# Attention with mixture of experts on one core: values of the last 64 queries in the same PSUM tile as those before, and two key chunks ahead of them

## The chip, the cores and the metric

The kernel runs on one core of one Trainium2 chip. The metric is the device time of one execution in microseconds; lower is better. Matrix work runs on TensorE (PE), with its weight loads shown as PEld; VectorE is DVE, ScalarE is ACT, GpSimd is POOL, and SP issues most of the DMAs.

## The reference

Everything is float32. There are 4 batches of 8 heads, 576 tokens and head dimension 64.

```python
scores = scale * np.matmul(q, k.transpose(0, 1, 3, 2))
bias = np.maximum((psi_rel / psi_i)[..., None] @ w1 + b1, 0.0) @ w2
scores = scores + bias.transpose(2, 0, 1)[None, :, :, :]
attn = softmax(scores)                  # over the keys, written out with max, exp and sum
x = np.matmul(attn, v)                  # then laid out as 2304 tokens by 512
e_idx = np.argmax(x @ w_gate, axis=1)   # one expert of 8 for each token
for e in range(8):
    h = np.maximum(x[mask] @ w1[e], 0.0)
    out[mask] = gate_w[mask, None] * eom[mask, e, None] * (h @ w2[e])
```

## The kernel before, in words

The program has three stages: the bias table, which the first pair of heads already overlaps; attention over 16 pairs of heads (a pair is a batch `b` and two heads `pr`, 4 pairs to a batch); and the experts. Attention is software pipelined over pairs. A loop over `n` from 0 to 16 reads a string of short operation names, and each name emits instructions on several engines in that order. `FIRST` is the string of n = 0, `ORDER` that of n = 1 to 14, `LAST` that of n = 15, `END` that of n = 16. Every engine then executes its own instructions strictly in the order of emission, so the string is the schedule. A name with `-` works on pair n-1, with `+` or `++` on pair n+1 or n+2.

The names that matter here:

- `s0` to `s7` (`emit_s`, scores): query block and head, two blocks of 288 keys. Four matmuls (L853) write a tile `ps`; DVE adds the bias and finds the row maximum (L833); ACT takes the exponential into a tile `e` (L838). `s5` and `s4` are the last scores of a pair, `s2` and `s1` the first of the next. `s8` is the same for the 64 queries that are left (L869).
- `t..` (`emit_t`): transposes of `e` on PE (L890, and L902 for the last 64 queries) into a tile `pt`, then a copy to SBUF. The last letter of a name tells the engine of the copy, `a` for ACT and `d` for DVE; in the last batch t00, t01, t04 and t14 are copied by ACT. In the part that changes these are `t14` (2 transposes), `t13` and `t00` (4 each) and `t21` (1, L902).
- `a0`, `a1`, `a2` (`emit_av`, values): `a0` and `a1` have 256 queries each, `a2` the last 64. Each is 20 matmuls (L922), 64 columns of the array wide, in two interleaved groups of partitions 0 to 63 and 64 to 127, into a tile `pa`, then one copy by ACT or DVE (L923).
- `k0`, `k1`, `k2` (`emit_kq`, key and query chunks of pair n+2): three transposes (L803) into `pt`, then ACT writes the rounded high part `hi` (L806), then DVE the low part `lo` from `pt` and `hi` (L808). Only then is `pt` free.
- `p0` to `p2` (`emit_place`): DMAs on SP that put `hi` and `lo` of pair n+1 where the scores need them (L819). `l` and `v` load keys, queries and values; `z` and `g` are small POOL copies.
- `w` and `u` (`do_work`): one step of the work that waits in a list, namely the gate logits of a finished batch (L586, L616, L628), its routing (small DVE and POOL operations), and the output rows (`emit_x`, 4 transposes L655 into `pt` and a DVE multiplication L664). `u` counts only from n = 12. A `w` step can be empty.

The pools: `ps` has 2 buffers, `pt` has 3 that are used in turn by all of `t`, `k` and the list's steps, and `pa` has one:

```python
ps_t = ctx.enter_context(tc.tile_pool(name="ps_t", bufs=3, space=PSUM))
ps_s = pool("ps_s", 2, space=PSUM)
ps_a = pool("ps_a", 1, space=PSUM)
```

Of the kernel before, what the change touches and what calls it, by code (L numbers as in the profile page):

```python
# [9 lines left out]
F32 = mybir.dt.float32  # L10
# [10 lines left out]
B, H, S, D = 4, 8, 576, 64  # L21
HID = 32
NPAIR = H // 2
# [22 lines left out]

ORDER = (
    "s2 s1 c w u a0d- t10a- p0+ s3 u w t11a- s0 u t12a- s6 t20d- p1+ u s7 b- t04d u s8 t01d t03a u "
    "t02a s5 s4 z+ u w w g- a1a- t14d u p2+ t13a t00d u k0++ a2a- v+ t21d u k1++ w k2++ u l+++ "
)  # L50

FIRST = (
# [82 lines left out]
def attention_moe_kernel(  # L135
# [15 lines left out]
    nc = tc.nc  # L151
# [404 lines left out]
    work = []  # L556
# [17 lines left out]
    def xt_of(b, qq):  # L574
        if (b, qq) not in xt_t:
            n = 256 if qq < 2 else 64
            nm = f"xt{int(qq == 2)}"
            xt_t[b, qq] = xt_p.tile([128, NPAIR, n], F32, name=nm, tag=nm, bufs=4 if qq < 2 else 2)
        return xt_t[b, qq]
# [92 lines left out]
    with ExitStack() as actx:  # L672
# [167 lines left out]
        def emit_s(b, pr, qb, hl):  # L840
            h = 2 * pr + hl
            if b not in sums_t:
                sums_t[b] = st_p.tile([128, 4, H], F32, name="sums", tag="sums", bufs=2)
                sums4_t[b] = st_p.tile([128, NPAIR], F32, name="sums4", tag="sums4", bufs=2)
            e_t[b, pr, qb] = e_all[qb]
            ps = ps_s.tile([128, 2, 512], F32, name="ps", tag="s")
            kt, qs = (x[(b * NPAIR + pr) % 2] for x in (kh2, qs2))
            low = kl_t[b, pr]
            o = hl * S + qb * 128
            k0 = hl * S  # L850
            for c in range(2):
                for n, keys in enumerate((kt, low)):
                    nc.tensor.matmul(  # L853
                        ps[:, c, 0:288], lhsT=qs[:, o:o + 128], rhs=keys[:, k0 + c * 288:k0 + c * 288 + 288],
                        start=n == 0, stop=n == 1,
                    )
            yield
            softmax_rows(e_t[b, pr, qb][:, hl, :], ps, bias[qb][:, h, :], sums_t[b][:, qb, h:h + 1])
# [45 lines left out]
                )  # L904
            copy(out=et[0:m, n0 * 128:(n0 + nn) * 128], in_=pt[0:m, 0:nn * 128])

        def emit_av(b, pr, qq, copy):
            et = et_t.pop((b, pr, qq))
            n = 256 if qq < 2 else 64
            vt, z = v_t[b, pr], vz[(b * NPAIR + pr) % 2]  # L910
            pa = ps_a.tile([128, 256], F32, name="pa", tag="a")
            if qq < 2:
                first = [(vt[:, i, :], et[:, i, :]) for i in range(4)] + [(z[:, 0, :], et[:, 4, :])]
                second = [(vt[:, 5 + i, :], et[:, 5 + i, :]) for i in range(4)] + [(z[:, 1, :], et[:, 4, :])]
            else:
                first, second = (
                    [(x[:, i, :], et[:, i, o:o + 64]) for i in range(4)] + [(y, et[:, 4, o:o + 64])]
                    for x, y, o in ((vt, z[:, 0, :], 0), (vb_t.pop((b, pr)), vz[2], 64))
                )
            for i in range(5):  # L920
                for p, (values, weights) in zip((0, 64), (first[i], second[i])):
                    nc.tensor.matmul(pa[p:p + 64, 0:n], lhsT=values, rhs=weights, start=i == 0, stop=i == 4)  # L922
            copy(out=xt_of(b, qq)[:, pr, :], in_=pa[:, 0:n])  # L923

        pairs = [(b, pr) for b in range(B) for pr in range(NPAIR)]
        begun = " ".join(BEGIN.values()).split()
# [20 lines left out]
        def finish(g):  # L947
            for _ in g:
                pass
# [44 lines left out]
        def copies(c):  # L994
            return nc.scalar.copy if c == "a" else V.tensor_copy
# [5 lines left out]
        for n in range(len(pairs) + 1):  # L1001
            todo = {i: 1 for i in range(8)}
            for op in orders.get(n, ORDER).split():
                name = op.rstrip("+-")
                m = n + op.count("+") - op.count("-")
                if name == "w":
                    do_work()
                elif name == "u" and n >= len(pairs) - NPAIR:
                    do_work((work,))
                elif name == "x":  # L1010
                    transpose_x(0, chunks.pop(0))
                elif name == "W":
                    first_w1()
                elif name == "B":
                    emit_load_vb(*pairs[-1])
                elif name == "X":
                    while any(w.__name__ == "route_group" for w in work):
                        do_work((work,))
                    first_x()
                elif name == "y":  # L1020
                    first_split(splits.pop(0))
                if name in "wuxWBXy" or not 0 <= m < len(pairs) or m == 0 and name in begun or m == 1 and name[0] == "p":
                    continue
                b, pr = pairs[m]
                i = int((name + "0")[1])
                if name == "s8":
                    emit_s4(b, pr)
                elif name[0] == "s":
                    finish(emit_s(b, pr, i // 2, i % 2))
                    if m == len(pairs) - 1:  # L1030

                        todo.pop(i)
                        if i > 5 and not any(j in todo for j in (6, 7)):
                            work.insert(0, first(first_w2))
                        if i in (4, 5) and not any(j in todo for j in (4, 5)):
                            t = biasp.tile([128, 4, 4, CH], F32R, name="x", tag="bias2")
                            xs.update({j: (t[:, 2 * j], t[:, 2 * j + 1]) for j in range(2)})
                elif name[0] == "t":
                    emit_t(
                        b, pr, i, int(name[2]), copies("a" if name[0:3] in to_act and b == B - 1 and m < len(pairs) - 1 else name[3])  # L1040
                    )
                elif name[0] == "a":
                    emit_av(b, pr, i, copies(name[2]))
                    if i == 2 and m == len(pairs) - 2:
                        emit_zb(*pairs[-1])
                    if pr == NPAIR - 1:
                        work.append(emit_logits(b, i))
                        if i == 2:
                            work.append(emit_route(b))
                            if b >= B - 2:  # L1050
                                work.append(route_group(b - (B - 2)))
                elif name[0] in "kp":
                    if name[0] == "p":
                        emit_place(b, pr, i)
                    else:
                        finish(emit_kq(b, pr, i))
                else:
                    {"l": emit_load, "v": emit_load_v, "c": emit_z, "b": emit_load_vb, "g": emit_zb, "z": emit_q4}[name](b, pr)
# [204 lines left out]
```

## Time and profile before

| | us |
|---|---|
| median of 3 runs | 620.95 |
| lowest and highest | 619.73, 623.54 |
| profiled execution | 615.56 |
| its span, first to last instruction | 613.4 |
| its mean granted PE clock, share of full speed | 0.987 |

The profile is of one execution, 615.56 us long, of which 613.4 us are the span and 2.16 us lie around it. Times in the rows are microseconds from the span's start. The matmul ends shown are modelled and overlap the next starts, so in this text a step on PE is measured from one start to the next start. A row `x10` merges ten neighbouring instructions of one kind.

### The profile page before, as it was taken

To read this page: it belongs to the slowest core of one execution; us is meant where nothing else is said; L and a number is where in the kernel's file an instruction comes from. 1 tells how busy PE (TensorE), PEld (TensorE's weight loads), DVE (VectorE), ACT (ScalarE), POOL (GpSimd) and SP (SyncE) were. 2 spreads that over 40 slices of the span, in tenths; PEclk is the share of its full clock that TensorE was granted. 3 is DMA by queue.
4 is the path that set the end of the run, shared out by engine and by line. 5 is a ranking of instruction groups with operands and counts; after the bars stand their busy time and mean duration, and the time that the engine had idled before them with its cause. 6 is when DMAs were issued, how large, how long until landed. Compare 5 with 4: busy or idle time off the path is not lost.

```text
span 613.4 us, 13534 instructions
## 1 busy us (share of the span) xinstructions
PE 575.6 (94%) x5070; PEld 489.3 (80%) x5070; DVE 413.5 (67%) x974; ACT 374.8 (61%) x774; POOL 94.9 (15%) x172
## 2 busy tenths in 40 slices
PE   4878789999999999999999999999999999999993
PEld 2333478887887788887778769999999999999993
DVE  6968656676786677786579765766777675555621
ACT  5778667777775677776776664545545454545410
POOL 1000000000001000100012383040404132220202
PEclk9979989999999999999999999999999999999998
DMA  6998975655656745676436686576656574855521
GB/s 144 226 207 207 215 161 116 139 125 108 143 127 169 167 99 108 137 184 157 105 88 158 185 263 198 172 221 204 202 179 203 172 221 145 241 166 182 174 71 47
DMA packets 99094, 100.26 MB, mean 163 GB/s; under 512 B 71320, under 2 KB 71576, under 8 KB 99017
## 3 DMA queue, kind: packets, MB, share of 16 engines
q1 hardware_dynamic: 93028, 84.93, 54.4%
q0 software_dynamic: 3232, 9.64, 5.0%
q10 hardware_dynamic: 2756, 4.72, 2.2%
q8 instruction: 42, 0.69, 0.5%
q14 instruction: 36, 0.29, 0.2%
HBM read 60.34 MB, written 9.50 MB: 114 GB/s over the span
## 4 chain that ended last, share of the span: by engine, by line
PE 79%; DVE 7%; ACT 5%; DMA 5%; issue 3%; POOL 0%; POOLq 0%; SPq 0%; DVEq 0%; ACTq 0%
PE p L1115 16%; PE p L1138 16%; PE pa L922 13%; PE ps L853 10%; PE pt L890 10%; PE pt L803 2%; DMA bias<-evh 2%; PE pb L735 2%; PE ps L869 2%; DVE e L833 2%; DVE hid L724 2%; PE pt L655 1%; PE pt L1157 1%; PE pt L902 1%; PE pt L515 1%
## 5 line engine op out<-in xcount | busy, mean ns | idle before, releaser
L838 ACT ACTIVATE e<-e,nm 128x576 f32<-128x576 f32 x144 | 111.2, 773 | 49.1 <-DVE nm L833 47.0
L833 DVE CUSTOM_DVE_ANT_0 e<-ps,bias 128x576 f32<-128x576 f32 x144 | 105.6, 751 | 31.3 <-PE ps L853 25.3
L1115 PE MATMUL p<-x,w 128*128 128x288 f32 x768 | 105.8, 297 | 0.0
L1115 PEld LDWEIGHTS p<-x,w 128*128 128x128 f32 x768 | 102.8, 188 | 0.5 <-issue 0.4
L890 PE MATMUL pt<-kept,e 128*128 128x128 f32 x576 | 82.7, 277 | 2.9 <-ACT et L894 1.6
L853 PE MATMUL ps<-qt,qs 128*128 128x288 f32 x256 | 79.9, 331 | 3.2 <-DVE nm L833 3.0
L890 PEld LDWEIGHTS pt<-kept,e 128*128 128x128 f32 x576 | 65.2, 141 | 17.8 <-issue 7.0
L1138 PE MATMUL p<-hh,w2h 128*128 128x288 f32 x256 | 77.4, 302 | 0.0
L1138 PE MATMUL p<-hl,w2h 128*128 128x288 f32 x256 | 75.7, 296 | 0.1
L1138 PE MATMUL p<-hh,w2l 128*128 128x288 f32 x256 | 75.4, 295 | 0.0
L922 PE MATMUL pa<-et,vt 128*64 128x256 f32 (+1 forms) x640 | 73.2, 354 | 0.0
L853 PE MATMUL ps<-kl,qs 128*128 128x288 f32 x256 | 71.3, 296 | 0.0
L894 ACT COPY et<-pt 128x512 f32<-128x512 f32 (+1 forms) x105 | 57.2, 565 | 12.4 <-PE pt L890 12.3
L735 PE MATMUL pb<-hid,w2blk 128*32 128x288 f32 x576 | 47.8, 442 | 17.3 <-DVE hid L724 7.4
L922 PEld LDWEIGHTS pa<-et,vt 128*64 128x64 f32 x640 | 42.6, 137 | 21.8 <-issue 6.0
L853 PEld LDWEIGHTS ps<-qt,qs 128*128 128x128 f32 x256 | 48.9, 191 | 7.2 <-DVE nm L833 4.5
L1117 ACT ACTIVATE hh<-p 128x288 fp32r<-128x288 f32 x64 | 26.3, 411 | 46.1 <-PE p L1115 38.0
L1080 POOL DMA_INDIRECT out_dram<-y,sidx x22 | 26.4, 1198 | 172.9 <-DVE y L1160 145.3
L735 PEld LDWEIGHTS pb<-hid,w2blk 128*32 128x32 f32 x576 | 19.1, 116 | 42.1 <-DVE hid L724 10.7
L724 DVE TENSOR_SCALAR hid<-e,early 128x576 f32<-128x576 f32 x110 | 48.4, 511 | 6.1 <-PE pb L735 2.8
L853 PEld LDWEIGHTS ps<-kl,qs 128*128 128x128 f32 x256 | 49.1, 192 | 0.0
L487 DVE TENSOR_TENSOR w2l<-w2r,w2h 128x1024 fp32r<-128x1024 f32 x32 | 39.2, 1225 | 14.5 <-ACT w2h L486 14.5
(218 smaller groups left out, 970.8 us busy)
## 6 DMA issues: line engine op xcount, KB each, us to landing
w1r<-in_moe_w_dram SPq DMA_DIRECT2D x36, 512.0 KB, 3.7
w2r<-in_moe_w_dram SPq DMA_DIRECT2D x36, 512.0 KB, 4.0
kl<-qs SPq DMA_DIRECT2D x32, 288.0 KB, 5.2
nat<-in_k_dram SPq DMA_DIRECT2D x16, 288.0 KB, 3.9
nat<-in_q_dram SPq DMA_DIRECT2D x16, 288.0 KB, 5.2
bias<-evh SPq DMA_DIRECT2D x16, 288.0 KB, 4.2
bias<-evl SPq DMA_DIRECT2D x16, 288.0 KB, 5.3
qs<-qt SPq DMA_DIRECT2D x16, 288.0 KB, 3.2
```

The source lines that it names most:

```text
L487: V.tensor_tensor(out=lo, in0=src, in1=hi.bitcast(F32), op=ALU.subtract)
L724: V.tensor_scalar(out=to, in0=src, scalar1=bc[:, r:r + 1], scalar2=0.0, op0=ALU.add, op1=ALU.max,)
L735: nc.tensor.matmul(pb[32 * t:32 * t + 32, c, 0:288], lhsT=w2f, rhs=hids[t][:, c * 288:c * 288 + 288], start=True, stop=True,)
L833: V.tensor_tensor_reduce(out=e.rearrange("p (a j) -> p a j", a=2), in0=ps[:, :, 0:n], in1=bias_ap.rearrange("p (a j) -> p a j", a=2), scal ...
L838: nc.scalar.activation(out=e, in_=e, func=ACTF.Exp, scale=-1.0, bias=nm, accum_out=sum_ap)
L853: nc.tensor.matmul(ps[:, c, 0:288], lhsT=qs[:, o:o + 128], rhs=keys[:, k0 + c * 288:k0 + c * 288 + 288], start=n == 0, stop=n == 1,)
L890: nc.tensor.transpose(pt[:, n * 256 + j * 128:n * 256 + j * 128 + 128], es[j][:, (n0 + n) * 128:(n0 + n) * 128 + 128], ident,)
L894: copy(out=et[:, n0:n0 + nn, :].rearrange("p n s -> p (n s)"), in_=pt[:, 0:nn * 256])
L922: nc.tensor.matmul(pa[p:p + 64, 0:n], lhsT=values, rhs=weights, start=i == 0, stop=i == 4)
L1080: p = nc.gpsimd.indirect_dma_start(out=out, out_offset=bass.IndirectOffsetOnAxis(ap=idx, axis=0), in_=y[0:n], in_offset=None, bounds_check ...
L1115: nc.tensor.matmul(p1[:, 0:CH], lhsT=w[:, fs], rhs=x[:, c, :], start=n == 0, stop=n == 11)
L1138: nc.tensor.matmul(p2[:, 0:CH], lhsT=w[f // 2][:, f % 2, ds], rhs=x[f], start=n == 0, stop=n == 23)
```

## The change

The string `ORDER` becomes, where it differs:

```diff
-    "t02a s5 s4 z+ u w w g- a1a- t14d u p2+ t13a t00d u k0++ a2a- v+ t21d u k1++ w k2++ u l+++ "
+    "t02a s5 z+ s4&k0++ k1++ u w w g- a12a- t14d u p2+ t13a t00d u k2++ v+ t21d u w u l+++ "
```

`a12` emits the matmuls of `a1` and then those of `a2`, both into one tile `pa` of 320 columns, and then both copies. `s4&k0` emits the matmuls of `s4`, the transposes and the ACT part of `k0`, then DVE and ACT of `s4`, then the DVE part of `k0`. `k1` follows, and only `k2` stays behind. `FIRST`, `LAST` and `END` stay as they are. At n = 14 there is no pair n+2, and neither kernel has a `k` there.

```diff
-        def emit_av(b, pr, qq, copy):
+        def emit_av(b, pr, qq, copy, pa, at):
             et = et_t.pop((b, pr, qq))
             n = 256 if qq < 2 else 64
             vt, z = v_t[b, pr], vz[(b * NPAIR + pr) % 2]
-            pa = ps_a.tile([128, 256], F32, name="pa", tag="a")
+            pa = pa[:, at:at + n]
...
-                    nc.tensor.matmul(pa[p:p + 64, 0:n], lhsT=values, rhs=weights, start=i == 0, stop=i == 4)
-            copy(out=xt_of(b, qq)[:, pr, :], in_=pa[:, 0:n])
+                    nc.tensor.matmul(pa[p:p + 64], lhsT=values, rhs=weights, start=i == 0, stop=i == 4)
+            yield
+            copy(out=xt_of(b, qq)[:, pr, :], in_=pa)
...
+                op, _, beside = op.partition("&")
...
-                    finish(emit_s(b, pr, i // 2, i % 2))
+                    steps = [emit_s(b, pr, i // 2, i % 2)]
+                    if beside and n + 2 < len(pairs):
+                        steps.append(emit_kq(*pairs[n + 2], int(beside[1])))
+                    for g in steps:
+                        next(g)
+                    for g in steps:
+                        finish(g)
...
-                    emit_av(b, pr, i, copies(name[2]))
...
+                    pa = ps_a.tile([128, 320], F32, name="pa", tag="a")
+                    qqs = [int(c) for c in name[1:-1]]
+                    begun_av = [emit_av(b, pr, i, copies(name[-1]), pa, 256 * j) for j, i in enumerate(qqs)]
+                    for g in begun_av:
+                        next(g)
+                    for i, g in zip(qqs, begun_av):
+                        finish(g)
```

On PE, from the end of `a1` to the next pair's scores at n = 1, the kernel before has these rows; `pt` numbers are single tiles, and what stands in brackets are the engines whose semaphores the row waits for.

```order
L890 MATMUL pt_1185<-kept_93,e0_136 128x128 [waits PE_49]
...
L803 MATMUL pt_1191<-kept_93,nat_1010 128x128 [waits DMAHW5_49,DMAHW4_49,DVE_49]
L803 MATMUL pt_1191<-kept_93,nat_1010 128x128 x2
L922 MATMUL pa_1197<-et4_892,vt_877 64x64 [waits Activation_49]
...
L902 MATMUL pt_1212<-kept_93,e4_891 64x128 [waits Activation_49]
L803 MATMUL pt_1215<-kept_93,nat_1010 128x128 [waits DVE_49]
L803 MATMUL pt_1215<-kept_93,nat_1010 128x128 x2
L803 MATMUL pt_1221<-kept_93,nat_1010 128x128 [waits DVE_49]
L803 MATMUL pt_1221<-kept_93,nat_1010 128x128 x2
L853 MATMUL ps_1230<-qt0_118,qs0_120 128x288 [waits DMAHW3_49,DMAHW0_49]
```

The changed kernel has these there, from `k0` (pt_1156) and `k1` (pt_1165) through the two kinds of values to `t14`, `t13`, `t00`, `k2`, `t21`.

```order
L803 MATMUL pt_1156<-kept_93,nat_1010 128x128 [waits DMAHW5_49,DMAHW4_49,DVE_49]
...
L803 MATMUL pt_1165<-kept_93,nat_1010 128x128 [waits Activation_49]
...
L922 MATMUL pa_1172<-et_977,vt_877 64x256 x8
...
L922 MATMUL pa_1172<-et4_892,vt_877 64x64
...
L890 MATMUL pt_1198<-kept_93,e2_138 128x128 [waits Activation_49]
L890 MATMUL pt_1203<-kept_93,e2_138 128x128 [waits DVE_49]
L890 MATMUL pt_1209<-kept_93,e0_136 128x128 [waits DVE_49]
L803 MATMUL pt_1215<-kept_93,nat_1010 128x128 [waits DVE_49]
L902 MATMUL pt_1223<-kept_93,e4_891 64x128 [waits Activation_49]
L853 MATMUL ps_1229<-qt0_118,qs0_120 128x288 [waits DMAHW3_49,DMAHW0_49]
```

Before, `k2` (pt_1221) takes the buffer of `k0` and waits for its DVE part, and `a2` waits for ACT's copy of `a1`. After, `t13` takes the buffer of `k0`, `t00` that of `k1`, `k2` that of `t14`, and `t21` that of `t13`, whose copy is ACT's.

On ACT, in the same stretch of n = 1, this piece of the difference shows what moved (L806 is the high part of a `k`, L838 the exponentials of `s5` and `s4`, L923 and L924 the copies of the values).

```order
-L838 ACTIVATE e_138,sums<-e_138,nm 128x576 x2
-L923 COPY xt_1171<-pa 128x256
-L894 COPY et<-pt 128x512
-L806 ACTIVATE qt_119<-pt,kept 128x384
-L923 COPY xt_1208<-pa 128x64
-L806 ACTIVATE qt_119<-pt,kept 128x384 x2
+L838 ACTIVATE e_138,sums<-e_138,nm 128x576
+L806 ACTIVATE qt_119<-pt,kept 128x384
+L838 ACTIVATE e_138,sums<-e_138,nm 128x576
+L806 ACTIVATE qt_119<-pt,kept 128x384
+L924 COPY xt_1193<-pa 128x256
+L924 COPY xt_1195<-pa 128x64
```

Two of the three L806 now stand around the exponential of `s4`, in front of both value copies, and the copy of `t13` follows these.

At n = 13 the two steps of the list before the values are both L655. Before, PE has them right behind the scores:

```order
L853 MATMUL ps_4029<-kl_3638,qs1_121 128x288
L655 MATMUL pt_4043<-kept_93,xt0_2903 128x128 [waits Activation_49]
L655 MATMUL pt_4043<-kept_93,xt0_2903 128x128 x3
L655 MATMUL pt_4050<-kept_93,xt0_2903 128x128 [waits Activation_49]
L655 MATMUL pt_4050<-kept_93,xt0_2903 128x128 x3
```

After, `k0` (pt_4023) and `k1` (pt_4032) precede them:

```order
L803 MATMUL pt_4023<-kept_93,nat_3841 128x128 [waits DMAHW3_49,DMAHW2_49,Activation_49]
L803 MATMUL pt_4023<-kept_93,nat_3841 128x128 x2
L803 MATMUL pt_4032<-kept_93,nat_3841 128x128 [waits Activation_49]
L803 MATMUL pt_4032<-kept_93,nat_3841 128x128 x2
L655 MATMUL pt_4043<-kept_93,xt0_2895 128x128 [waits Activation_49]
L655 MATMUL pt_4043<-kept_93,xt0_2895 128x128 x3
L655 MATMUL pt_4050<-kept_93,xt0_2895 128x128 [waits DVE_49]
```

The second L655 now waits for DVE, which is the low part of `k0`, since that held the buffer.

## Rows read from the trace of the kernel before

**Rows 1.** The page: busy time, share of the span and instructions of each engine
```profile
PE 575.6 (94%) x5070; PEld 489.3 (80%) x5070; DVE 413.5 (67%) x974; ACT 374.8 (61%) x774; POOL 94.9 (15%) x172
```

**Rows 2.** Windows: length, busy PE, PEld, DVE, ACT, POOL, clock, DMA, GB/s
```profile
100.00:120.00 20.00, 19.93 (x189) 16.63 (x189) 13.84 (x34) 14.70 (x33) 0.98 (x4) 1.00 0.59 128
420.00:500.00 80.00, 80.00 (x628) 79.97 (x627) 59.48 (x136) 39.81 (x72) 20.83 (x18) 1.00 0.59 185
```

**Rows 3.** Timeline of PE, s5 at n = 2 to the next scores: start, length
```profile
111.59 0.38 PE L853 MATMUL ps<-qt,qs 128*128 128x288 f32 x1
...
112.82 1.95 PE L922 MATMUL pa<-et,vt 128*64 128x256 f32 x16
114.60 0.60 PE L922 MATMUL pa<-et,vz 128*64 128x256 f32 x4
115.13 1.31 PE L890 MATMUL pt<-kept,e 128*128 128x128 f32 x10
116.28 0.49 PE L803 MATMUL pt<-kept,nat 128*128 128x128 f32 x3
116.70 0.27 PE L922 MATMUL pa<-et,vt 128*64 128x64 f32 x1
...
117.43 0.30 PE L902 MATMUL pt<-kept,e 128*64 128x128 f32 x1
117.57 1.07 PE L803 MATMUL pt<-kept,nat 128*128 128x128 f32 x6
118.40 0.38 PE L853 MATMUL ps<-qt,qs 128*128 128x288 f32 x1
```

**Rows 4.** Timeline of ACT in the same stretch
```profile
112.25 1.05 ACT L894 COPY et<-pt 128x512 f32<-128x512 f32 x2
113.32 0.77 ACT L838 ACTIVATE e<-e,nm 128x576 f32<-128x576 f32 x1
...
116.10 0.59 ACT L894 COPY et<-pt 128x512 f32<-128x512 f32 x1 [0.48 <-PE pt L890]
116.81 0.58 ACT L806 ACTIVATE qt<-pt,kept 128x384 fp32r<-128x384 f32 x1
```

**Rows 5.** Timeline of DVE in the same stretch
```profile
113.20 0.75 DVE L833 CUSTOM_DVE_ANT_0 e<-ps,bias 128x576 f32<-128x576 f32 x1
...
116.48 0.69 DVE L894 COPY et<-pt 128x512 f32<-128x512 f32 x1 [0.45 <-PE pt L890]
117.42 0.62 DVE L808 SCALAR_TENSOR_TENSOR qs<-pt,kept,qt 128x384 fp32r<-128x384 f32 x1 [0.25 <-ACT qt L806]
```

**Rows 6.** Timeline of PE at n = 6
```profile
182.79 0.60 PE L655 MATMUL pt<-kept,xt 128*128 128x128 f32 x4
183.32 1.95 PE L922 MATMUL pa<-et,vt 128*64 128x256 f32 x16
...
187.23 0.66 PE L890 MATMUL pt<-kept,e 128*128 128x128 f32 x4 [0.73 <-ACT et L894]
```

**Rows 7.** Timeline of PE at n = 14, t21 and the next scores
```profile
340.70 0.30 PE L902 MATMUL pt<-kept,e 128*64 128x128 f32 x1
340.75 0.38 PE L853 MATMUL ps<-qt,qs 128*128 128x288 f32 x1
```

**Rows 8.** Timeline of PE at n = 13, s5 to the next scores
```profile
314.68 0.38 PE L853 MATMUL ps<-qt,qs 128*128 128x288 f32 x1
...
315.82 1.03 PE L655 MATMUL pt<-kept,xt 128*128 128x128 f32 x8
...
323.00 0.38 PE L853 MATMUL ps<-qt,qs 128*128 128x288 f32 x1
```

**Rows 9.** Timeline of ACT at n = 13, the exponential of s5
```profile
316.40 0.78 ACT L838 ACTIVATE e<-e,nm 128x576 f32<-128x576 f32 x1 [0.85 <-DVE nm L833]
```

**Rows 10.** Issue of the last placing DMA for the next pair; landing times by kind
```profile
113.48 0.46 SPq L819 DMA_DIRECT2D qt<-qt  x1
...
qs<-qt SPq DMA_DIRECT2D x16, 288.0 KB, 3.2
```

More of the change, by code (lines that the diff above doesn't have):

```diff
@@ L1042, in attention_moe_kernel @@
                 elif name[0] == "a":
-                    emit_av(b, pr, i, copies(name[2]))
[L1044 to L1051, printed above, removed]
+                    pa = ps_a.tile([128, 320], F32, name="pa", tag="a")
[5 more added lines that the diff above has]
+                        finish(g)
+                        if i == 2 and m == len(pairs) - 2:
+                            emit_zb(*pairs[-1])
+                        if pr == NPAIR - 1:
+                            work.append(emit_logits(b, i))
+                            if i == 2:
+                                work.append(emit_route(b))
+                                if b >= B - 2:
+                                    work.append(route_group(b - (B - 2)))
                 elif name[0] in "kp":
```

## The prediction

> **What bounds the kernel now.** The page comes first: PE is busy 94% of the span, DVE 67%, ACT 61% [rows 1]. The windows then show where: in the attention stage PE is busy 19.93 of 20 us at full clock, and in the expert stage 80.00 of 80 [rows 2]. A busy PE in this view can still be held up, since matmul ends are modelled and overlap. So the third view is the timeline of PE, read from start to start, through the stretch that the change rebuilds: from the scores s5 and s4 (111.59) to the next pair's scores (118.40) are 6.81 us [rows 3]. What PE saves or loses there it passes on, because everything later in attention is paced by PE, and the experts behind it leave PE no idle time that could swallow it.
>
> Three step sizes are hidden in that stretch. Ten transposes (L890) take 1.15 us, so 0.11 each [rows 3]. Four transposes of L655 in front of the values take 183.32 - 182.79 = 0.53 [rows 6]; without three steps of 0.11 that leaves 0.20 for the step from a transpose to the values. Inside a run of values, 16 instructions take 114.60 - 112.82 = 1.78 us, which is 8 pairs of 0.22 [rows 3]. The last two pairs would end at 115.03; the transposes start at 115.13, so leaving the values costs 0.10, and the x10 row behind them holds some 0.06 more than ten steps.
>
> **The change part by part, on PE.** All for a pair without work from the list.
>
> Scores: eight L853 followed by values take 1.23 us [rows 3], followed by transposes 1.14 [rows 8]. Now k0 and k1 follow: 1.14.
>
> k0 and k1 before the values: five steps of 0.11 and one of 0.20 are 0.75.
>
> a1 followed by a2 without a change of shape: 2.31 - 0.10 = 2.21. No row shows 256-column and 64-column values back to back. The ends are 2.10 (nothing at all between them, less than the ten pairs) and 2.31 (as if it left the values); I take 2.21, since neither the weight shape nor the partition groups change.
>
> a2 took 117.43 - 116.70 = 0.73 [rows 3]. Its first pair holds an extra 0.05 for entering, which a1 now pays: 0.68.
>
> t14, t13, t00 stay at 1.15 behind values. k2: 3 x 0.11 = 0.33. t21 to the next scores: 0.05 [rows 7].
>
> Sum: 1.14 + 0.75 + 2.21 + 0.68 + 1.15 + 0.33 + 0.05 = 6.31, against 6.81. So 0.50 is saved if PE waits for nothing. Half of it is one entry and one exit of the values' shape. The other half is a wait that goes: six L803 (k1 and k2) take 118.40 - 117.57 = 0.83, where 5 x 0.11 + 0.03 = 0.58 would do; in the middle DVE ends k0's low part at 117.42 + 0.62 = 118.04 [rows 5], and k2 needs that buffer.
>
> **What is late next.** I follow the three `pt` buffers in the new order, with s5's start as zero. ACT ends the copies of t03 and t02 at 1.71 and starts s5's exponential at 1.73 [rows 4]. Behind it now stand k0's high part (0.58, from 2.50), s4's exponential (0.77), k1's high part (3.85 to 4.40). DVE ends s4's maximum at 2.36 [rows 5], then waits: k0's low part ends near 3.7, k1's near 5.0. PE wants k0's buffer for t13 at 1.14 + 0.75 + 2.21 + 0.68 + 0.27 = 5.05 and k1's for t00 at 5.49. Both are free, the second with 0.5 us to spare. The value copies, first and second, wait in ACT's queue for the end of a2, at about 4.85; behind them stands t13's copy, which cannot start before 5.7, so they are hidden. k2 takes t14's buffer, which DVE frees in time.
>
> t21 is the one that waits. t13's copy ends about 0.95 us after its last transpose starts: 116.10 + 0.59 = 116.69, against 115.13 + 0.06 + 5 x 0.11 = 115.74 for the sixth of the x10 [rows 3, 4]. Four transposes of t00 and three of k2 lie between, so t21 is due after 8 x 0.11 = 0.87 us. It waits about 0.13 with the semaphore's delay. A pair without work of the list saves 0.50 - 0.13 = 0.37. There are seven: n = 1, 2, 3, 5, 7, 9, 11 (at 5, 7, 9 and 11 the list has at most steps that cost the same in both orders). Together 2.6 us.
>
> At n = 4, 6, 8, 10 the last `w` has matmuls that need a `pt`. It moves from between k1 and k2 to behind t21, and the buffer is then t00's. DVE's copy of t00 takes 0.69 [rows 5] and frees it 1.01 us after t00's last transpose starts; PE is there after 0.55. That wait of some 0.45, in place of the old 0.25, plus the steps, uses up the 0.50: I put them at zero, -0.1 each at 4 and 8. At n = 6 there is something extra: t00 starts at 187.23 after 0.73 us of visible idle [rows 6], which by its start-to-start step (1.00 against 0.11) is 0.9 us, waiting for ACT's copy of t13. In the new order t00 waits there for DVE alone, which is done. That gives 0.9.
>
> The last batch goes the other way. At n = 13 both `w` steps before the values are output rows. The second needs k0's buffer. ACT starts s5's exponential there at 316.40, 1.72 after s5 [rows 8, 9]; with 0.77 for it, 0.58 for the high part and 0.6 for the low part the buffer is free at 3.7, and PE is there at 1.14 + 0.65 + 0.44 = 2.23. So a stall of 1.45 stands right in front of the values; set against the 0.50 minus waits of the tail, n = 13 loses 1.3 (it now takes 323.00 - 314.68 = 8.32 [rows 8]). At n = 12 the list's last step, a logits step that needs a buffer, stands behind t21 and gets k2's: k2's high and low part, 1.2 us in a row behind ACT's copies, are then waited for, where the old order had k1 and k2 to put between. I take -0.6, with -1.2 and 0 as ends. At n = 14 no k moves and only the joined values remain: +0.2.
>
> DMA: the next pair's last placing is issued at 113.48 and lands about 3.2 later, at 116.7 [rows 10], 1.7 us before the scores that need it. The new order brings these scores 0.37 forward, and the chain of placings starts from k2, which is 0.6 earlier too. Nothing becomes late.
>
> Sum: 2.6 - 0.2 + 0.9 - 1.3 - 0.6 + 0.2 = 1.6 us saved, 0.26%. On the profiled execution's own time that is 615.56 - 1.6 = 614.0. The runs that are compared lie higher, with a median 5.4 above that execution, so the forecast on their scale is 620.95 - 1.6 = 619.3.
>
> **The rivals.**
>
> No new waits. If t21, the last `w` and n = 12 and 13 find their buffers free, all fourteen pairs save 0.50, and n = 6 another 0.9: 7.9 us, 613.0. For it: ACT is only 14.70 of 20 us busy [rows 2]. Against it: the copy of t13 is fixed by PE's own order, not by load. Chance 0.10.
>
> Slower: the two chunks' evacuation comes too late for PE. Its place is t13 and t00, right behind the joined values. k1's low part has 0.5 us to spare; that margin is made of five ACT steps and two DVE steps in a row. From 0.5 us of delay on, PE stalls in every pair with a chunk. If it comes 1.2 us later than I have it, each of 13 pairs stalls 0.7 and its 0.37 becomes -0.2; with the last batch 13 x 0.2 + 1.7 - 0.9 = 3.4 us are lost, 624.4. For it: ACT has its longest unbroken run just there, from 112.25 on [rows 4]. Against it: the times above already include that run. Chance 0.17, and 0.05 that it is bad enough for more than 1%.
>
> t21 costs a switch of its own. Row by row, t21 is an operation 64 columns wide like the values, and it stood directly behind a2. Now it has 128-column transposes before it and scores behind it. If entering and leaving it cost 0.10 each as the values do [rows 3], the seven pairs save 0.17 instead of 0.37, and the other pairs lose 0.2 each: 14 x 0.2 = 2.8 less saved, 1.2 us slower than before, 622.2. Against it: t21 to the scores takes 0.05 where a weight of the same width precedes [rows 7], and t21 to the transposes 117.57 - 117.43 = 0.14, near an ordinary step [rows 3]. The Trainium skill (TensorEngine Tiling (Array Packing), Key Properties) says that a change of tiling mode drains the engine; by that rule the number of drains would be four before and four after, if t21 counts as the narrow mode. The trace agrees for the values (0.10 out), not for t21. Chance 0.13.
>
> **How the numbers follow.** The forecast has 0.60, the rivals 0.10, 0.17 and 0.13. The forecast's own bounds: 0.2 to 0.5 for the seven pairs (1.4 to 3.5), the value step between 2.10 and 2.31 (14 x 0.1 = 1.4 either way), and the last batch between 0 and -2.5. That gives 616 to 621.5; the rivals on both sides and the scatter of the runs (619.73 to 623.54) widen it to 615.0 to 623.3. Within 1% (about what a measurement of this kernel can tell from no change) lie 614.7 to 627.2: the forecast and nearly all of the second and third rivals. Faster by more: the first rival, 0.10. Slower by more: 0.06.
>
> **What would show it.** In the changed profile, start to start from s5 to the next scores at n = 2 should be 6.4 us; L922 should show the 64-column values 2.21 behind the first; t21 should start about 1.0 after t13's last transpose, with ACT's copy as releaser; at n = 6 the 0.73 should be gone; at n = 13 the second L655 should wait more than 1 us for L808. The prediction is wrong if PE stalls at t13 or t00 in ordinary pairs, if t21 shows a step above 0.1 on either side without a wait, or if n = 13 shows no stall.

## The result, and the profile after

| | before | after |
|---|---|---|
| median of 14 runs, us | 621.01 | 624.22 |
| lowest and highest | 618.12, 624.59 | 622.61, 627.10 |
| profiled execution, its span | 615.56, 613.4 | 624.89, 622.7 |

The ratio after to before is 1.0052, with a 95% interval of 1.0030 to 1.0074. The forecast was 619.3, from 615.0 to 623.3: within 1% as said, but on the wrong side, and above the range.

The page of the changed kernel and the two windows hardly differ from [rows 1, 2]: a busy share does not show where 3 us went.

```profile
PE 576.8 (93%) x5070; PEld 493.7 (79%) x5070; DVE 414.0 (66%) x974; ACT 370.2 (59%) x774; POOL 94.8 (15%) x172
```

```profile
100.00:120.00 20.00, 20.00 (x190) 17.26 (x188) 14.10 (x34) 14.10 (x33) 0.99 (x4) 1.00 0.61 129
420.00:500.00 80.00, 80.00 (x630) 79.94 (x629) 58.41 (x129) 40.36 (x71) 16.58 (x14) 1.00 0.62 194
```

What shows it is the start of s8 (the first L869) in each pair, from one pair to the next. For n = 5 these are the rows, first of the kernel before (17.13 us apart), then of the changed one (17.80).

```profile
162.15 0.40 PE L869 MATMUL ps<-qt,q 128*128 128x288 f32 x1
...
179.28 0.38 PE L869 MATMUL ps<-qt,q 128*128 128x288 f32 x1
```

```profile
162.13 0.40 PE L869 MATMUL ps<-qt,q 128*128 128x288 f32 x1
...
179.93 0.38 PE L869 MATMUL ps<-qt,q 128*128 128x288 f32 x1
```

The same for all pairs, with the saving that was forecast and the one measured (minus is a loss):

| n | before | after | forecast | measured |
|---|---|---|---|---|
| 1, 2, 3 | 16.81, 16.84, 17.57 | 16.50, 16.51, 17.27 | 0.37 each | 0.31, 0.33, 0.30 |
| 4, 8, 10 | 18.54, 18.53, 18.57 | 18.62, 18.62, 18.60 | -0.1, -0.1, 0 | -0.08, -0.09, -0.03 |
| 5 | 17.13 | 17.80 | 0.37 | -0.67 |
| 6 | 19.50 | 18.62 | 0.9 | 0.88 |
| 7 | 18.02 | 18.00 | 0.37 | 0.02 |
| 9 | 17.12 | 18.13 | 0.37 | -1.01 |
| 11 | 18.91 | 18.86 | 0.37 | 0.05 |
| 12 | 20.69 | 21.18 | -0.6 | -0.49 |
| 13 | 21.35 | 22.86 | -1.3 | -1.51 |
| 14 | 20.03 | 19.82 | 0.2 | 0.21 |
| sum, 1 to 14 | 259.60 | 261.39 | 1.6 | -1.79 |

Four pairs carry the miss: n = 5, 7, 9 and 11 came out 1.04, 0.35, 1.38 and 0.32 us worse than forecast, 3.1 of the 3.4 between the two sums.

An ordinary pair went as worked out. PE at n = 2, answering to [rows 3]:

```profile
112.12 0.38 PE L853 MATMUL ps<-qt,qs 128*128 128x288 f32 x1
...
113.26 0.82 PE L803 MATMUL pt<-kept,nat 128*128 128x128 f32 x6
114.01 1.95 PE L922 MATMUL pa<-et,vt 128*64 128x256 f32 x16
...
116.22 0.22 PE L922 MATMUL pa<-et,vt 128*64 128x64 f32 x1
...
116.90 1.31 PE L890 MATMUL pt<-kept,e 128*128 128x128 f32 x10
118.05 0.49 PE L803 MATMUL pt<-kept,nat 128*128 128x128 f32 x3
118.51 0.30 PE L902 MATMUL pt<-kept,e 128*64 128x128 f32 x1
118.61 0.37 PE L853 MATMUL ps<-qt,qs 128*128 128x288 f32 x1
```

From start to start: 1.14, 0.75, 2.21, 0.68, 1.15, then 0.46 for k2 with t21's wait, 0.10; together 6.49 instead of 6.81.

The pair n = 5 has list work: a logits step and the first step of the routing. PE there, and DVE and ACT behind it:

```profile
169.44 1.31 PE L890 MATMUL pt<-kept,e 128*128 128x128 f32 x10
171.23 0.55 PE L803 MATMUL pt<-kept,nat 128*128 128x128 f32 x3 [0.48 <-DVE et L894]
172.02 0.30 PE L902 MATMUL pt<-kept,e 128*64 128x128 f32 x1 [0.25 <-ACT et L894]
```

```profile
168.93 0.62 DVE L808 SCALAR_TENSOR_TENSOR qs<-pt,kept,qt 128x384 fp32r<-128x384 f32 x1 [0.68 <-ACT qt L806]
169.46 0.27 DVE L630 TENSOR_TENSOR lt<-pt,rec 64x128 f32<-64x128 f32 x1
169.77 0.37 DVE L634 TENSOR_REDUCE logits<-lt 64x16 f32<-64x128 f32 x1
...
170.64 0.20 DVE L205 SCALAR_TENSOR_TENSOR oh<-sh,kept 128x40 f32<-128x40 f32 x1
170.75 1.01 DVE L894 COPY et<-pt 128x256 f32<-128x256 f32 x2
```

```profile
170.87 0.24 ACT L209 ACTIVATE sh<-sh 128x40 f32<-128x40 f32 x1 [2.04 <-DVE oh L205]
171.01 0.47 ACT L924 COPY xt<-pa 128x256 f32<-128x256 f32 x2
171.37 0.60 ACT L894 COPY et<-pt 128x512 f32<-128x512 f32 x1
```

The list's five DVE operations stand behind k1's low part, which waits for ACT. t14's copy stands behind them and starts at 170.75, though t14 was transposed at 169.6; k2 takes t14's buffer, so the ten transposes and the step to k2 take 171.23 - 169.44 = 1.79 instead of 1.15. On ACT the routing's exponential waits for the same five operations, and both value copies and t13's copy wait behind it; t21 needs t13's buffer and comes 0.79 after k2 instead of 0.46. These two, 0.64 and 0.33, make up the 0.99 by which n = 5 falls short of an ordinary pair's saving of 0.32. In the kernel before, the same operations ran on DVE from 166.82 to 168.2, right behind the maximum of s4, in time in which DVE had nothing else:

```profile
166.82 0.28 DVE L630 TENSOR_TENSOR lt<-pt,rec 64x128 f32<-64x128 f32 x1
...
168.00 0.20 DVE L205 SCALAR_TENSOR_TENSOR oh<-sh,kept 128x40 f32<-128x40 f32 x1
168.66 0.42 DVE L894 COPY et<-pt 128x256 f32<-128x256 f32 x1 [0.47 <-PE pt L890]
```

At n = 9 a part is of another kind. DVE and PE of the changed kernel there:

```profile
242.30 0.62 DVE L808 SCALAR_TENSOR_TENSOR qs<-pt,kept,qt 128x384 fp32r<-128x384 f32 x1 [1.04 <-ACT qt L806]
```

```profile
242.44 1.63 PE L890 MATMUL pt<-kept,e 128*128 128x128 f32 x10
244.60 0.55 PE L803 MATMUL pt<-kept,nat 128*128 128x128 f32 x3 [0.53 <-DVE et L894]
```

k1's low part starts 0.47 after its high part has ended (0.10 at n = 5) and ends at 242.92. t13, due at 242.71, starts at 242.97: the ten transposes hold a wait of 0.26 for the low part itself. The profile does not show what holds the low part up; profiles of issue_on_pool and issue_on_pool_g, two later kernels with the same order of k0, k1 and the list steps, have the same 0.47.

### The profile page after: what moved, and what is told of

The parts are those of the page before. It is cut to its first block, busy times and chain, and to the rows that moved or that the text cites. A ratio compares the mean times of both kernels' runs of the same rounds, so it can differ in the third digit from the quotient of the medians.

```text
span 622.7 us, 13537 instructions
## 1 busy us (share of the span) xinstructions
PE 576.8 (93%) x5070; PEld 493.7 (79%) x5070; DVE 414.0 (66%) x974; ACT 370.2 (59%) x774; POOL 94.8 (15%) x172
## 4 chain that ended last, share of the span: by engine, by line
PE 73%; DVE 9%; ACT 7%; issue 5%; DMA 4%; POOL 0%; POOLq 0%; SPq 0%; ACTq 0%; DVEq 0%; another core or an unknown queue 0%
PE p L1152 16%; PE p L1129 15%; PE pa L922 11%; PE ps L853 9%; PE pt L890 8%; PE pb L735 4%; DVE e L833 3%; ACT e L838 2%; PE ps L869 2%; ACT et L894 2%; PE pt L1171 1%; DMA bias<-evl 1%; PE pt L515 1%; PE pt L803 1%; DMA bias<-evh 1%
## 5 line engine op out<-in xcount | busy, mean ns | idle before, releaser
L838 ACT ACTIVATE e<-e,nm 128x576 f32<-128x576 f32 x144 | 111.3, 774 | 52.5 <-DVE nm L833 50.7
L1129 PE MATMUL p<-x,w 128*128 128x288 f32 x768 | 107.8, 299 | 1.6 <-issue 1.5
L1129 PEld LDWEIGHTS p<-x,w 128*128 128x128 f32 x768 | 104.4, 190 | 2.4 <-issue 2.3
L735 PE MATMUL pb<-hid,w2blk 128*32 128x288 f32 x576 | 49.8, 466 | 17.2 <-DVE hid L724 7.7
L735 PEld LDWEIGHTS pb<-hid,w2blk 128*32 128x32 f32 x576 | 21.1, 122 | 42.3 <-DVE hid L724 10.9
L808 DVE SCALAR_TENSOR_TENSOR qs<-pt,kept,qt 128x384 fp32r<-128x384 f32 x48 | 29.6, 617 | 31.7 <-ACT qt L806 31.7
```

Source lines behind the costliest of these rows:

```text
L735: nc.tensor.matmul(pb[32 * t:32 * t + 32, c, 0:288], lhsT=w2f, rhs=hids[t][:, c * 288:c * 288 + 288], start=True, stop=True,)
L808: V.scalar_tensor_tensor(out=lo, in0=pt[:, 0:384], scalar=cn("ksc"), in1=hi.bitcast(F32), op0=ALU.mult, op1=ALU.subtract)
L838: nc.scalar.activation(out=e, in_=e, func=ACTF.Exp, scale=-1.0, bias=nm, accum_out=sum_ap)
L1129: nc.tensor.matmul(p1[:, 0:CH], lhsT=w[:, fs], rhs=x[:, c, :], start=n == 0, stop=n == 11)
```

## The experiments

Theory A: the loss lies in the pairs with list work; the list's steps now stand behind the low parts of k0 and k1 in the queues of DVE and ACT, and what PE needs stands behind them. Rivals: the joined tile `pa` costs; the low parts are too late by themselves; the loss lies in the first expert slot. s8 to s8 in the profiles of the first six kernels (before_again is the kernel before once more); the sum is that of n = 1 to 14, from the s8 of pair 1 to that of pair 15 (the expectations call it the fifteen pairs):

| n | before | before_again | after | list_ahead | front_alone | join_alone | list_last |
|---|---|---|---|---|---|---|---|
| 2 | 16.84 | 16.84 | 16.51 | 16.49 | 16.82 | 17.43 | 16.49 |
| 5 | 17.13 | 17.13 | 17.80 | 17.05 | 18.24 | 17.70 | 17.05 |
| 7 | 18.02 | 18.02 | 18.00 | 18.02 | 18.45 | 18.60 | 17.26 |
| 8 | 18.53 | 18.54 | 18.62 | 18.69 | 18.95 | 19.14 | 20.11 |
| 9 | 17.12 | 17.16 | 18.13 | 17.25 | 18.58 | 17.73 | 16.91 |
| 13 | 21.35 | 21.34 | 22.86 | 22.08 | 23.06 | 21.95 | 20.43 |
| sum | 259.60 | 259.67 | 261.39 | 259.08 | 266.21 | 266.18 | 265.75 |

**The kernel before, once more** (no edit).

> The kernel before, unchanged, for a second profile of it and for the scatter. Theory A (the loss of the changed kernel lies in attention, at pairs with list work; the 5.4 us more that its first expert slot took in the one profile are chance): the slot's time from the first L1115 to the first L1138, 14.7 us in the first profile of the kernel before and 20.1 us in the changed kernel, is not fixed and can come out long here too; every s8-to-s8 distance of the pairs repeats within 0.1 us (17.13 at n = 5, 17.12 at n = 9). Theory B (the slot's loss belongs to the change): 14.7 again. Ratio 1.000 within its interval for both.

621.31 against 620.62, ratio 1.0008 (0.9984 to 1.0033). The distances repeat within 0.04 us. The first expert slot took 18.55 us this time, not 14.71, and two kernels with k0 and k1 in front took 18.49 and 18.53 on the same chip (list_ahead and front_alone, below). So the 5.4 us between 14.71 and the 20.11 of the changed kernel's profile cannot be charged to the change. More on that slot below.

**List steps between s5 and s4.**

```diff
-    "t02a s5 z+ s4&k0++ k1++ u w w g- a12a- ..."
+    "t02a s5 u w w z+ s4&k0++ k1++ g- a12a- ..."
```

> The changed kernel with the two list steps between s5 and s4, so that their DVE parts stand in front of the low parts of k0 and k1. Theory A: n = 5 falls from 17.80 to about 16.85, n = 9 from 18.13 to about 16.85, n = 7 and n = 11 lose their k2 wait (18.00 to 17.7, 18.86 to 18.6), n = 13 loses the 1.6 us stall of the second L655 (22.86 to about 21.3); n = 12 stays near 21.2, since its late step is the last one. Together 4.7 us less than the changed kernel, about 619.5. Rival (the two kinds of values in one tile, with both copies behind both, make t13 and the rest late): n = 5 and n = 9 stay at 17.8 and 18.1, and the time stays at 624.

619.76, ratio to before 0.9977 (0.9952 to 1.0002), so not clearly faster than the kernel before. The two pairs that lost most get 0.75 and 0.88 us back, with the joined tile unchanged, so the joined tile is not the cause. At n = 5 the ten transposes are ordinary again:

```profile
167.46 1.35 PE L890 MATMUL pt<-kept,e 128*128 128x128 f32 x10
168.64 0.49 PE L803 MATMUL pt<-kept,nat 128*128 128x128 f32 x3
169.06 0.30 PE L902 MATMUL pt<-kept,e 128*64 128x128 f32 x1
```

Half of the expected 4.7 us is missing: by the pairs 2.3 came, so the median's nearness to the expected 619.5 is chance. At n = 9 the ten transposes still take 1.55, since t00 waits 0.35 for k1's low part. n = 7 and 11 did not move: t21's wait went, but k2 waits there instead, for t13's copy. At n = 13 the second L655 no longer waits for k0's low part; k1 waits some 0.8 us for that L655's multiplication.

```profile
204.81 0.55 PE L803 MATMUL pt<-kept,nat 128*128 128x128 f32 x3 [0.29 <-ACT et L894]
```

```profile
315.38 0.55 PE L803 MATMUL pt<-kept,nat 128*128 128x128 f32 x3 [0.60 <-DVE x L664]
```

**Each half of the change alone.** First k0 and k1 in front, the last 64 queries' values behind t00:

```diff
-    "... a12a- t14d u p2+ t13a t00d u k2++ v+ ..."
+    "... a1a- t14d u p2+ t13a t00d u a2a- k2++ v+ ..."
```

> k0 and k1 in front of the values as in the changed kernel, but the last 64 queries' values apart, behind t00, with their own tile. Theory A: the losses at n = 5, 9 and 13 come from the low parts standing in front of the list's DVE steps, so they stay in kind (a few tenths smaller, because the 64-column values give k2 0.7 us more); ordinary pairs (n = 1, 2, 3) save the k2 wait, 0.26 us of 6.81, instead of the 0.31 of the changed kernel. Rival (the joined tile is the cause): n = 5 and n = 9 are at or below 17.1. Time about 624 by theory A, 619 by the rival.

Then the values joined, with k0, k1 and k2 behind them:

```diff
-    "t02a s5 z+ s4&k0++ k1++ u w w g- a12a- t14d u p2+ t13a t00d u k2++ v+ t21d u w u l+++ "
+    "t02a s5 s4 z+ u w w g- a12a- t14d u p2+ t13a t00d u k0++ v+ t21d u k1++ w k2++ u l+++ "
```

> The values joined, the three chunks behind them as before, nothing in front. Theory A: k2 now comes 0.7 us sooner behind k0, whose low part it needs, and t21 sooner behind t13; ordinary pairs lose the 0.25 us of the joined values again and about 0.4 more at k2 (6.81 becomes about 7.2), but n = 5, 9 and 13 show no loss of their own, because the list's DVE steps keep their place. Together 12 to 14 pairs by 0.4, about 5 us slower than before, 626. Rival (the joined tile is the cause at n = 5 and 9): these two pairs lose 0.7 and 1.0 here too, more than the ordinary ones.

626.62, ratio 1.0105 (1.0060 to 1.0150), and 630.17, ratio 1.0118 (1.0071 to 1.0164), where 624 and 626 were expected. Neither half gains anything in an ordinary pair: 16.82 and 17.43 at n = 2, against 16.84 before and 16.51 with both. For k0 and k1 in front I expected 0.26 saved and got 0.02. The two rows show why: k1's low part ends at 115.69 + 0.62 = 116.31, and t00, due at 116.21, waits for it. The ten transposes and the step into the values take 1.45 us; 1.15 and 0.09 more for entering the values would be 1.24, so the wait costs 0.21.

```profile
115.69 0.62 DVE L808 SCALAR_TENSOR_TENSOR qs<-pt,kept,qt 128x384 fp32r<-128x384 f32 x1 [0.68 <-ACT qt L806]
```

```profile
115.50 1.52 PE L890 MATMUL pt<-kept,e 128*128 128x128 f32 x10
...
116.95 0.27 PE L922 MATMUL pa<-et,vt 128*64 128x64 f32 x1
```

With the values joined, 0.68 us of them stand ahead of t14, and that is the cover of the low parts. Joined alone, they leave the place between k0 and k2, and PE waits for t00's copy at k1 and for k0's low part at k2:

```profile
118.17 0.55 PE L803 MATMUL pt<-kept,nat 128*128 128x128 f32 x3 [0.19 <-DVE et L894]
119.03 0.55 PE L803 MATMUL pt<-kept,nat 128*128 128x128 f32 x3 [0.32 <-DVE qs L808]
```

At n = 5 and 9 joining alone loses 0.57 and 0.61, just what it loses at n = 2 (0.59, where about 0.4 was expected). So the joined tile costs nothing of its own there; the losses at n = 5, 9 and 13 come with k0 and k1 in front. front_alone has them, but larger (1.11, 1.46 and 1.71 against the kernel before), where I expected them a few tenths smaller.

**List steps last.**

```diff
-    "... k1++ u w w g- a12a- t14d u p2+ t13a t00d u k2++ v+ t21d u w u l+++ "
+    "... k1++ u g- a12a- t14d u p2+ t13a t00d u k2++ v+ t21d u w w u w l+++ "
```

> The changed kernel with all three list steps behind t21, so that nothing of the list stands on DVE between the low parts and the copies of t14 and t00. Theory A (the list's DVE steps behind the low parts delay t14's, t00's and t13's copies): the ten transposes at n = 5 and n = 9 take 1.15 again instead of 1.79 and 2.16; what is paid in its place is the wait for t00's buffer behind t21, 0.4 us, and at n = 13 a second and third L655 that wait for k2's low part and each other, 1.5 us or more. n = 5 and 9 about 17.2, n = 13 about 22.9, the whole about 621 to 623. Rival (the low parts themselves are too late for t14 and t00 at these pairs): the ten transposes stay above 1.5 us.

631.67, ratio 1.0141 (1.0107 to 1.0175). The ten transposes at n = 5 and 9 take 1.15 us, so with no list work in that place the low parts are in time. It is a weaker test than meant, since in this order the list had no step left at those two places, and it does not clear the low part at n = 9 of the changed kernel, where the wait of 0.26 is seen. The price was far above my estimate: at n = 4 and 8 three logits steps in a row behind t21 wait for buffers and for ACT, 1.5 us more a pair, and n = 14 takes 24.54 instead of 19.82. n = 13, expected at 22.9, took 20.43.

**The changed order only where it gains.** The order of the kernel before is kept as a second string:

```diff
+        orders.update((n, APART) for n in (4, 5, 7, 8, 9, 10, 11, 12, 13))
```

> The changed kernel's order only at n = 1, 2, 3, 6 and 14, the order of the kernel before at the other pairs. If the gain of the change is local to pairs without list work and its loss local to the others, the pairs do not influence each other: n = 1, 2, 3 keep 16.50, 16.51 and 17.27, n = 6 keeps 18.62 and n = 14 19.82, all others go back to the numbers of the kernel before (17.13, 17.12, 21.35 at n = 5, 9, 13). From s8 to s8 over the fifteen pairs that is 259.6 - 2.0 = 257.6 us, so 2.0 us below the kernel before (0.3%) and 3.8 below the changed kernel. Rival (what a pair gains is given back by the next one): no more than 1 us below the kernel before.

In the second kernel n = 4, 6, 8 and 10 have the changed order with the list step in front of t21:

```diff
+EARLY_W = ORDER.replace("u k2++ v+ t21d u w u", "u k2++ w v+ t21d u u")
...
+        orders.update((n, APART) for n in (5, 7, 9, 11, 12, 13))
+        orders.update((n, EARLY_W) for n in (4, 6, 8, 10))
```

> As by_pair, but n = 4, 6, 8 and 10 have the changed order with the last list step between k2 and t21, so that it takes t13's buffer (ACT's copy) and t21 takes t00's. The 0.39 us that PE waits in the changed kernel behind t21 for DVE's copy of t00 should shrink to about 0.13 in front of the list step; n = 4, 8 and 10 then take about 18.4, n = 6 18.4. Together 0.75 us below by_pair, 256.9 us over the fifteen pairs. Rival: t21 or the next scores wait in place of the list step, and the four pairs stay at 18.6.

The sums are 257.67 and 256.70 us (expected 257.6 and 256.9): in these two orders the pairs do not influence each other. Measured ratios: 0.9954 (0.9936 to 0.9972) and 0.9955 (0.9930 to 0.9980); the further 1.0 us of the second is seen in the pairs, not in the medians.

**ACT's queue at n = 7 and 11.** There the list has the last output rows of a batch, and their store (L670) is issued by ACT. In the changed kernel ACT, then PE, at n = 7:

```profile
204.66 0.56 ACT L806 ACTIVATE qt<-pt,kept 128x384 fp32r<-128x384 f32 x1
206.49 0.51 ACTq L670 DMA_DIRECT2D x_dram<-x  x1
207.04 0.49 ACT L924 COPY xt<-pa 128x256 f32<-128x256 f32 x2 [1.82 <-PE pt L890]
```

```profile
207.31 0.49 PE L803 MATMUL pt<-kept,nat 128*128 128x128 f32 x3
208.07 0.30 PE L902 MATMUL pt<-kept,e 128*64 128x128 f32 x1 [0.28 <-ACT et L894]
```

```diff
-        nc.scalar.dma_start(**stored)
+        nc.gpsimd.dma_start(**stored)
```

> The changed kernel with the last store of a batch's output rows (L670) issued by POOL instead of ACT. Theory A for n = 7 and n = 11: ACT's queue holds that store between k1's high part and the value copies; it waits for DVE's multiplication, which stands behind k1's low part, so the value copies and t13's copy start 0.85 us late and t21 waits 0.4 us longer. Without it n = 7 falls from 18.00 to about 17.65 and n = 11 from 18.86 to about 18.5, the 0.37 us forecast; n = 5 and n = 9, where ACT holds an exponential of the routing and DVE's copy of t14 is late by itself, stay at 17.8 and 18.1. Rival (at n = 7 and 11 it is DVE's multiplication in front of t14's copy that costs): both stay within 0.1 of 18.00 and 18.86.

> by_pair_early_w with that store on POOL and the changed order at n = 7 and n = 11 too. If the pairs are independent and theory A holds for ACT's queue, n = 7 takes about 17.65 and n = 11 about 18.5, all others as in by_pair_early_w: 256.7 - 0.75 = 255.95 us over the fifteen pairs, 3.7 us below the kernel before, 0.6%. Rival: no gain at n = 7 and 11, 256.7.

Both missed: n = 7 took 19.42 and 19.44, n = 11 20.33, and the ratios were 1.0094 (1.0062 to 1.0127) and 0.9997 (0.9979 to 1.0015). The store held up POOL instead of ACT: the small copy `g`, which the last values need, stands behind it.

```profile
204.42 0.59 POOL L670 DMA_DIRECT2D x_dram<-x  x1 [4.35 <-DVE x L664]
205.01 0.25 POOL L787 COPY vz<-vb 64x64 f32<-64x64 f32 x1
```

```profile
205.31 0.33 PE L922 MATMUL pa<-et,vz 128*64 128x64 f32 x2 [1.42 <-POOL vz L787]
```

So the same two kernels with `g` ahead of the list steps:

```diff
-    "... k1++ u w w g- a12a- ..."
+    "... k1++ g- u w w a12a- ..."
```

> As issue_on_pool, with the POOL copy g in front of the two list steps, since the store on POOL held up that copy (1.42 us, n = 7) and the last values with it. Theory A for ACT's queue at n = 7 and 11, which issue_on_pool could not test: n = 7 about 17.65, n = 11 about 18.5; all other pairs as in the changed kernel. Rival (DVE's multiplication in front of t14's copy costs there): both within 0.1 of 18.00 and 18.86. The first expert slot, 14.7 us in both profiles of the last chip and 18.5 to 22.1 on the others, is expected to go with the chip, not with the kernel.

> As by_pair_pool, with g in front of the two list steps. 255.95 us over the fifteen pairs if theory A holds, 256.7 if not; 3.7 or 2.9 us below the kernel before on the same chip.

n = 7 takes 17.75 and 17.69, n = 11 18.59 and 18.60: 0.25 to 0.31 us at each is what the store in ACT's queue had cost (`g` was moved too, but PE does not wait for `g` at n = 7 of the changed kernel). In the first of the two kernels n = 5 and 9, which keep the changed order there, stay at 17.78 and 18.15. Ratios 1.0032 (1.0020 to 1.0043) and 0.9947 (0.9931 to 0.9964). But the sum of the second kernel is 257.03, above both values that were expected, because n = 6 went back to 19.56 and 19.26: t00 waits there for ACT's copy of t13 again, as in [rows 6]. PE at n = 6, first in the changed kernel, then in issue_on_pool_g:

```profile
187.54 1.31 PE L890 MATMUL pt<-kept,e 128*128 128x128 f32 x10
```

```profile
187.69 0.66 PE L890 MATMUL pt<-kept,e 128*128 128x128 f32 x4 [0.73 <-ACT et L894]
```

In the program's order the row's wait has changed from DVE to ACT, though nothing of n = 6 but `g`, which uses no `pt`, was moved. I read it as the pool handing t00 the buffer of t13, on which the 0.88 us at n = 6 then hang; strictly in turn t00 would not get the buffer of the tile just before it, and the buffers themselves were not traced.

**`g` ahead at n = 7 and 11 alone.**

```diff
+EARLY_G = ORDER.replace("u w w g- a12a-", "g- u w w a12a-")
...
+        orders.update((n, EARLY_G) for n in (7, 11))
```

> As by_pair_pool_g, but g stands in front of the list steps only at n = 7 and 11. In the two runs before, moving g at every pair changed which buffer the pool gives t00 at n = 6: it waited for ACT's copy of t13 again, as in the kernel before (19.5 instead of 18.6). If that is all that went wrong there, n = 6 takes 18.3 again, n = 7 and 11 keep 17.7 and 18.6, and the fifteen pairs take 256.1 us, 3.5 us below the kernel before. If n = 6 stays at 19.3, the store on POOL is the cause and not g.

n = 6 takes 18.32, n = 7 and 11 17.66 and 18.59, the sum is 256.23. So the wait at n = 6 came with `g`, moved there or in an earlier pair, and not with the store. 611.87 against 615.45 for the kernel before on the same chip: ratio 0.9940 (0.9920 to 0.9960).

## Why the prediction was wrong

**The step that failed** is the bracket "at 5, 7, 9 and 11 the list has at most steps that cost the same in both orders". On PE they do. Their other parts do not: on DVE they now stand behind two low parts that wait for ACT, and in front of t14's copy; on ACT an exponential or a store that waits for them stands in front of the value copies and t13's copy. The place was priced at a saving of 0.37 a pair; it measured -0.67, 0.02, -1.01 and 0.05. At n = 9, 0.26 of the loss is k1's low part itself, and why it starts late there is open. I followed the three `pt` buffers through this very chain for a pair without list work, and priced list steps on DVE and ACT only where they take a buffer (n = 13). Taking the steps out of that place (list_ahead) gave back 0.75 and 0.88 us at n = 5 and 9; taking the store out of ACT's queue (issue_on_pool_g) 0.25 and 0.27 at n = 7 and 11.

**Ordinary pairs**: right. The values back to back took the 2.21 that I chose between 2.10 and 2.31, a2 0.68, k0 and k1 0.75. k1's low part ended at 116.51 + 0.62 = 117.13, 0.48 us before t00 was due, where 0.5 was worked out. Off was the last term: t21 to the scores took 0.10, not 0.05, so 0.31 was saved for 0.37.

```profile
116.51 0.62 DVE L808 SCALAR_TENSOR_TENSOR qs<-pt,kept,qt 128x384 fp32r<-128x384 f32 x1 [0.68 <-ACT qt L806]
```

**n = 4, 8, 10, 12 and 14, and the 0.88 at n = 6**: right within 0.11. At n = 4 and 8 part of that is luck: k2 waits 0.20 there for t14's copy, t21 for nothing and the list step behind it 0.16, where 0.13 at t21 and 0.45 at the list step were worked out. The 0.88 came by the wait that was named, but it hung on an order of buffers that moving `g` undid. At n = 13 the second L655 waits for k0's low part, as said:

```profile
317.80 0.60 PE L655 MATMUL pt<-kept,xt 128*128 128x128 f32 x4
319.77 0.65 PE L655 MATMUL pt<-kept,xt 128*128 128x128 f32 x4 [1.38 <-DVE qs L808]
```

**The rivals.** "No new waits" fell. "The two chunks' evacuation comes too late" has the right place for front_alone, where t00 waits for k1's low part, and for n = 9 of the changed kernel (0.26), but not for its ordinary pairs. That its time, 624.4, lies beside the measured 624.22 is chance (and its -0.2 a pair holds only if the stall of 0.7 also takes away the 0.13 at t21; from the 0.37 that it names, it would be -0.33). "t21 costs a switch of its own" fell: in front_alone, where t21 waits for nothing on PE's side, it starts 0.11 after k2's last transpose and the scores start 0.03 behind it. The 0.10 behind t21 in the changed kernel comes where t21 has waited; behind k2's first transpose, which waits at n = 5, the step is longer too (0.16 instead of 0.11). The Trainium skill (TensorEngine Tiling (Array Packing), Key Properties) says that changing the tiling mode drains the engine. These rows show no such price for one 64-column transpose among 128-column ones; whether that is a change of mode in the page's sense, no run shows.

```profile
118.06 0.27 PE L902 MATMUL pt<-kept,e 128*64 128x128 f32 x1
118.09 0.38 PE L853 MATMUL ps<-qt,qs 128*128 128x288 f32 x1
```

Every sign that the prediction named as deciding came out as said or close to it: 6.49 for 6.4 at n = 2, 2.21, t21 1.00 behind t13's last transpose and 0.06 after ACT's copy of t13 has ended (its row names no releaser), no 0.73 at n = 6, 1.38 at n = 13. The list of signs was at fault, since it named only ordinary pairs, n = 6 and n = 13.

**From the profile to the median.** The pairs lose 1.8 us, the medians differ by 3.2, with an interval of 1.9 to 4.6. So the pairs show why the time rose instead of falling, but 621.0 + 1.8 = 622.8 would still lie in the range. The two profiled executions differ by 9.3, mostly for other reasons: 5.4 are the slot below and 0.9 the stretch ahead of it. The 1.4 us more in the medians are not accounted for: the first s8 of pair 1, before which no kernel here differs in its order, came anywhere from 90.5 to 94.4 us, and the slot below scatters by as much.

## What to carry to other kernels

A step that is moved ahead in the program is moved ahead in every engine's queue; what must be listed is not only who waits for it, but who stood behind that place in each queue, in every iteration that has extra work, and a store that an engine issues counts as one of them. Two edits can be worth nothing apart and something together, when one is the cover of the other: test the halves before crediting either. Where an order is written per iteration, keep each iteration's better one: here that alone turned a loss of 0.5% into a gain of 0.5% (by_pair), and moving single steps in some pairs brought 0.6%.

## What the runs showed of the hardware

The first expert slot, from its first matmul (L1115 before, L1129 after) to the first of the second layer, has no edit in it. It took 14.71 or 14.72 us in the five profiles from three chips, 18.5 to 22.1 in the seven from two others. The five are all of kernels with the store on POOL, but the first profile of the kernel before, with the store on ACT, has 14.71 too, so the store does not decide it (on which chip that profile and the changed kernel's own were taken is not recorded). The medians of the kernel before went along, 615.0 to 615.6 on the first three chips, 620.6 and 622.2 on the other two, so I take it for the chip. The stretch ahead of the slot, from the s8 of pair 15, goes the same way: 18.19 us in the six profiles with the short slot, 19.07 to 19.23 in the other eight. The prediction read the 5.4 us between its profile and the timed runs as an offset; by the second profile of the kernel before 18.55 - 14.71 = 3.8 of it are this slot and 1.0 are the stretch ahead of it. DVE in the slot, first in the changed kernel's own profile (20.11 us), then in issue_on_pool_g (14.72):

```profile
379.55 0.22 DVE L924 COPY xt<-pa 128x64 f32<-128x64 f32 x1 [5.48 <-remote]
```

```profile
372.11 0.21 DVE L924 COPY xt<-pa 128x64 f32<-128x64 f32 x1
```

The copy, whose values PE had made ready by 373.8, starts 5.5 us late, and the profile names no engine of the core as its releaser. The DMA view of the changed kernel shows POOL's gathers on q0 from 374.0 to 379.5 (322 of 323 packets), and from 379.8 to 382.8 no packet at all. In the profile of before_again the copy came at 376.22, again as the gathers ended. That the gathers hold it up, and why on some chips only, was not tried.
